# A written order for all five queues, from batch 1's stage 1 to the first channel mixing, in a three-stage kernel on one core

## The chip, the cores and the metric

The kernel runs on 1 core of a Trainium2 chip. The metric is the device time of one execution in microseconds (us). The engines are PE (TensorE matmuls; PEld is its weight load), DVE (VectorE), ACT (ScalarE), POOL (GpSimd) and SP (SyncE, which issues the DMAs). Each engine takes its instructions in one fixed order and stops at the first one whose inputs or buffers are not ready.

## The reference, cut to what matters

```python
def reference(q, k, v, moe, moe2):          # all float32, batch 2, 8 heads, 768 positions, 64 wide
    x = _attn_ref(q, k, v)                   # stage 1: window of 16 and 24 block maxima as keys
    x = x.transpose(0, 2, 1, 3).reshape(2, 768, 512)
    x = _moe_ref(x, **moe)                   # stage 2: 4 experts, best 2 per position
    return _moe2_ref(x, **moe2)              # stage 3

def _moe_ref(x, w_gate, wq, wk, wv, wo):
    ...
    for e in range(E):
        q = x @ wq[e]
        k = x @ wk[e]
        v = x @ wv[e]
        scores = scale * (q @ k.transpose(0, 2, 1))
        scores = np.where(causal, -1000000000.0, scores)
        a = np.exp(scores - scores.max(-1, keepdims=True))
        a /= a.sum(-1, keepdims=True) + 1e-09
        ye = a @ v @ wo[e]
        ...                                  # out += weight of expert e at this position * ye

def _moe2_ref(x, w_tok1, w_tok2, w_ch1, w_ch2):
    xt = x.transpose(0, 2, 1)
    h = np.maximum(xt @ w_tok1, 0.0) @ w_tok2      # token mixing
    u = x + h.transpose(0, 2, 1)
    h2 = np.maximum(u @ w_ch1, 0.0) @ w_ch2        # channel mixing, 1536 wide
    return (u + h2).astype(np.float32)
```

The four weights of stage 3 come as float64 words; the kernel turns their bits into float32 itself ("decode" below).

## The kernel before, in words

All stages are in `stack_kernel`. Exact products are made of three matmuls: `mm3` (lines 112 to 114) multiplies high and low halves, which `split` (L104 on ACT, L105 on DVE) makes from a PSUM tile or from SBUF.

- Stage 1 (`s1_...`, lines 157 to 290): windowed attention, 12 groups per batch. Scores `s1s` (PE, L217), minima `mn` (DVE, L227), exponentials (ACT, L236), scaling (POOL, L252), transposes, value products `s1a` (PE, L271). Batch 0 follows the table FIRST; batch 1 is a generator.
- Stage 2: `proj` makes V, the gate weights `wg` and, in four tiles `pj` per batch and pair of experts, q and k; a tile's halves are called `s...h` and `s...l`, and SP copies them by DMA into q, k and k2l (L449, L450, L453). `attn` runs 8 units per batch (4 experts x 2 halves of the positions). A unit: scores `s2s` (PE, L476), mask and minimum into `pr` and `mn` (DVE, L481), exponential into `pr` with its sum `sm` (ACT, L486), `sm` plus a small number (POOL, L488), reciprocal `f` (DVE, L489), three scalings of `pr` by `f` and `wg` (POOL, L492), transposes `s2p` (PE, L502), split into `ph`/`pl` or copied whole as `pf` (ACT L506), products with V into `s2a` (PE, L507, L512, L513), sum into `yT` (ACT L516, DVE L517).
- Stage 3: `tokmix` makes `yh`/`yl`, `yt`/`nh`/`nl`, `z`, `g` and `u`, tile by tile. `chmix` makes `h` and `o` in four chunks of 384 channels for each batch and half of the positions; the weights of a chunk (`c1h`, `c1l`, `c2h`, `c2l`) come from `load_ch`.
- A decode (`decode_w`, lines 130 to 153) of 128x512 words: DMA into `raw` (L140, SP), absolute value `deca` (ACT, L143), clamp (POOL, L144), three integer steps (DVE, L145 to L147), low word (ACT, L149), product and sum (POOL, L150, L151), high half (ACT, L152), low half (POOL, L153). There are two buffers `raw` and two `deca`, shared by all weights.

Two things set the order. `run` (near line 610) takes turns among generators by their share of work done; after that a scheduler places the traced instructions on each queue as their inputs come, by times of its own. The runs are: stage 1 of batch 1 with `proj(0)`; `attn(0)` with `proj(1)` and the decode of the token weights; `attn(1)` with `tokmix(0)`, the first channel chunk's decode (`load_ch(0)`), the first `chpass` and `tokmix(1)`; then the remaining chunks.

Of the kernel before, what the change touches and what calls it, by code (L numbers as in the profile page):

```python
# [790 lines left out]
```

## Time and profile before

| what | value |
|---|---|
| time, median of 3 runs (lowest to highest) | 466.64 us (465.47 to 469.15) |
| time of the profiled execution | 467.73 us |
| its span (first to last instruction) | 465.9 us |
| granted TensorE clock | 0.998 of full speed |
| PE busy | 445.1 us, 96% of the span |
| PE weight loads busy | 420.7 us, 90% |
| DVE, ACT, POOL busy | 280.1, 231.2, 285.2 us (60, 50, 61%) |

Busy time is the union of an engine's instructions. PE instructions overlap, so a busy PE may still be short of its best rate. A wait is idle time of an engine right before an instruction, put down to the event that came last.

### The profile page before, as it was taken

The page shows a single profiled execution, that of the slowest core. Times are in us where ns is not written, and L with a number is a line of the kernel's source. Part 1 is how long each engine was busy: PE and PEld are TensorE (multiplying, and loading weights), DVE is VectorE, ACT ScalarE, POOL GpSimd, SP SyncE. Part 2 cuts the span into 40 slices and gives each one's busy share as a digit, 9 for nine tenths or more (in the row PEclk, how much of TensorE's full clock was granted, in tenths as well). Part 3 has the DMA queues.
Part 4 walks back from the last instruction along what each step waited for, and adds up shares of the span by engine and source line. Part 5 has one row for each costly group of instructions (what it writes and reads, how often), then busy time and mean ns, then how long its engine had stood idle before and what let it go on. Part 6 is the DMA issues. An engine that isn't in the chain of part 4 may idle for free.

```text
span 465.9 us, 8565 instructions
## 1 busy us (share of the span) xinstructions
PE 445.1 (96%) x3038; PEld 420.7 (90%) x3038; DVE 280.1 (60%) x818; ACT 231.2 (50%) x653; POOL 285.2 (61%) x319
## 2 busy tenths in 40 slices
PE   7899899999989878999999999999999999999996
PEld 7798789989978766897999999999999999999996
DVE  5573766759699679868773743677572673332322
ACT  4685665977778687885664423233323321111010
POOL 4568542768989887997873869877864771000000
PEclk9999999999999999999999999999999999999999
DMA  7999917806515865021111120212121100001111
GB/s 222 275 255 310 289 39 207 182 2 167 127 46 152 210 171 146 3 91 45 45 47 46 66 70 2 84 53 78 58 91 45 62 32 0 1 0 69 68 70 68
DMA packets 28522, 46.51 MB, mean 100 GB/s; under 512 B 2496, under 2 KB 19648, under 8 KB 28480
## 3 DMA queue, kind: packets, MB, share of 16 engines
q1 hardware_dynamic: 28480, 45.97, 35.2%
q8 instruction: 24, 0.39, 0.4%
q14 instruction: 18, 0.15, 0.1%
HBM read 33.38 MB, written 3.15 MB: 78 GB/s over the span
## 4 chain that ended last, share of the span: by engine, by line
PE 68%; DMA 10%; DVE 7%; POOL 4%; ACT 3%; issue 3%; SPq 3%; DVEq 0%; ACTq 0%; POOLq 0%
PE h L113 7%; PE h L112 7%; PE h L114 7%; PE o L112 7%; PE o L113 7%; PE o L114 7%; DMA kx<-in_kwT_dram 5%; PE s1s L217 4%; PE s1a L271 2%; DMA qb<-in_qT_dram 2%; POOL pr L492 2%; PE u L112 2%; PE pj L112 2%; PE u L113 2%; PE u L114 2%
## 5 line engine op out<-in xcount | busy, mean ns | idle before, releaser
L144 POOL TENSOR_SCALAR deca<-deca 128x512 f32<-128x512 f32 x30 | 58.0, 1938 | 10.5 <-ACT deca L143 9.7
L113 PE MATMUL o<-hl,c2h 128*128 128x384 f32 x192 | 64.2, 337 | 0.0
L114 PE MATMUL o<-hh,c2l 128*128 128x384 f32 x192 | 64.0, 336 | 0.0
L108 ACT ACTIVATE hh<-h 128x384 fp32r<-128x384 f32 x48 | 23.3, 490 | 79.4 <-PE h L114 78.8
L109 DVE SCALAR_TENSOR_TENSOR hl<-h,hh 128x384 fp32r<-128x384 f32 x48 | 26.5, 555 | 53.2 <-ACT hh L108 53.2
L605 DVE TENSOR_TENSOR oa<-o,oa 128x384 f32<-128x384 f32 x64 | 31.9, 550 | 38.5 <-PE o L114 38.5
L112 PE MATMUL o<-hh,c2h 128*128 128x384 f32 x192 | 49.4, 336 | 0.0
L236 ACT ACTIVATE pr<-n,mn 128x120 f32<-128x120 f32 x96 | 36.6, 384 | 16.3 <-DVE mn L227 15.8
L150 POOL TENSOR_TENSOR raw<-raw 128x512 f32<-128x512 f32 x30 | 31.3, 1042 | 20.4 <-DVE raw L147 18.6
L492 POOL TENSOR_SCALAR pr<-pr,f,wg 128x128 f32<-128x128 f32 (+5 forms) x48 | 40.1, 849 | 5.1 <-DVE f L489 2.9
L151 POOL TENSOR_TENSOR deca<-deca,raw 128x512 f32<-128x512 f32 x30 | 40.8, 1360 | 1.0
L149 ACT ACTIVATE raw<-raw 128x512 f32<-128x512 uint32 x30 | 20.3, 677 | 36.3 <-DMA raw<-in_ch_dram 25.6
L145 DVE TENSOR_SCALAR deca<-deca 128x512 int32<-128x512 int32 x30 | 27.8, 928 | 14.9 <-POOL deca L144 14.9
L486 ACT ACTIVATE pr<-pr,mn 128x128 f32<-128x128 f32 (+5 forms) x48 | 31.9, 665 | 9.8 <-DVE mn L481 9.7
L113 PEld LDWEIGHTS o<-hl,c2h 128*128 128x128 f32 x192 | 36.0, 188 | 0.3 <-DVE hl L109 0.3
L114 PEld LDWEIGHTS o<-hh,c2l 128*128 128x128 f32 x192 | 36.0, 188 | 0.0
L112 PEld LDWEIGHTS o<-hh,c2h 128*128 128x128 f32 x192 | 34.8, 188 | 0.1
L113 PE MATMUL h<-u0l,c1h 128*128 128x384 f32 x96 | 32.5, 338 | 0.0
L112 PE MATMUL h<-u0h,c1h 128*128 128x384 f32 x96 | 32.4, 338 | 0.0
L114 PE MATMUL h<-u0h,c1l 128*128 128x384 f32 x96 | 32.3, 337 | 0.0
L112 PE MATMUL h<-u1h,c1h 128*128 128x384 f32 x96 | 32.3, 336 | 0.0
L113 PE MATMUL h<-u1l,c1h 128*128 128x384 f32 x96 | 32.3, 336 | 0.0
(207 smaller groups left out, 1315.1 us busy)
## 6 DMA issues: line engine op xcount, KB each, us to landing
raw<-in_ch_dram SPq DMA_DIRECT2D x24, 512.0 KB, 3.5
kx<-in_kwT_dram SPq DMA_DIRECT2D x7, 720.0 KB, 10.0
vx<-in_vw_dram SPq DMA_DIRECT2D x8, 576.0 KB, 11.1
qb<-in_qT_dram SPq DMA_DIRECT2D x16, 192.0 KB, 8.9
raw<-in_tok_dram SPq DMA_DIRECT2D x6, 512.0 KB, 4.6
out_dram<-oa SPq DMA_DIRECT2D x16, 192.0 KB, 2.0
vt<-in_vT_dram SPq DMA_DIRECT2D x4, 384.0 KB, 10.3
rqk<-in_wqkv_dram SPq DMA_DIRECT2D x4, 256.0 KB, 10.2
```

What stands on the lines that cost most here:

```text
L109: vec.scalar_tensor_tensor(lo, src, 0.0, hi.bitcast(F32), op0=ALU.max, op1=ALU.subtract)
L112: ten.matmul(out, lh, rh, start=start, stop=False)
L113: ten.matmul(out, lh, rl, start=False, stop=False)
L114: ten.matmul(out, ll, rh, start=False, stop=stop)
L144: gps.tensor_scalar(af, af, F64_TINY, F64_HUGE, op0=ALU.max, op1=ALU.min)
L145: vec.tensor_scalar(ta, ta, 3, 0x3FFFFFFF, op0=ALU.logical_shift_left, op1=ALU.bitwise_and)
L150: gps.tensor_mul(lf, lf, ef)
L151: gps.tensor_add(af, af, lf)
L236: act.activation(pr[:, i, :], n[:, i, :], AF.Exp, bias=mn[:, i:i + 1], scale=-1.0, accum_out=sm[:, i:i + 1])
L486: act.activation(prs[r], prs[r], AF.Exp, bias=mn[:, r, ci:ci + 1], scale=-1.0, accum_out=sm[:, r:r + 1])
L492: gps.tensor_scalar(prs[r][:, :nk], prs[r][:, :nk], f[:, r:r + 1], wg[:, 3 * h + r, e:e + 1], op0=ALU.mult, op1=ALU.mult)
L605: vec.tensor_add(oa[d], a[:, :HALF], oa[d])
```

## The change: one table that orders all five queues

At the end of `stack_kernel` the traced instructions of each queue are taken in the order in which the program issues them and are chained, one to the next, in the order of a table of numbers. The chain carries no semaphore: it only tells the scheduler which instruction stands behind which. The instructions, the SBUF buffers and the arithmetic are the same; PSUM tiles take their banks in the new order. The table's order differs from the one before from about 63 us of the profile (stage 1 of batch 1) to the first chunk of channel mixing; behind it and ahead of it every queue reads as before.

```diff
+ORDER = {
+    "PE": """
+0-192 253-257 193-216 258-262 281-284 263-265 298-301 217-219 306-311 220-236 269-271 330-332 285 237-244 266-268
...
+    "DVE": """
...
+    "ACT": """
...
+    "POOL": """
...
+    "SP": """
+0-35 39 70 75 38 37 36 40 46-47 41 45 42 44 49 43 48 54 51 50 56 52-53 55 57 60 58-59 61 76 66 63 62 64-65 69 68 77 67
...
+}
...
+    queues = {"PE": ten, "DVE": vec, "ACT": act, "POOL": gps, "SP": nc.sync}
+    traced = list(nc.cur_bb.bb.instructions)
+    for name, table in ORDER.items():
+        mine = [x for x in traced if x.engine == queues[name].engine and type(x).__name__.startswith("Inst")]
+        places = []
+        for run_ in table.split():
+            a, _, z = run_.partition("-")
+            places += range(int(a), int(z or a) + 1)
+        assert sorted(places) == list(range(len(mine))), (name, len(places), len(mine))
+        for a, z in zip(places, places[1:]):
+            tc.add_manual_dep(mine[z], mine[a].name, NOSYNC, reason="keep_in_program_order")
     psa_cm.__exit__(None, None, None)
```

The table takes 107 lines at the top, so a line of the kernel before stands 107 lower in the rows of the changed one (L140 is L247 there, L492 is L599). In the rows below a tile's name ends in its number; `raw64` is the tile called `raw` in the profile, and `pr512`, `pr640`, `pr768` and so on are `pr` of that width.

**SP, where the last copies of k for experts 2 and 3 of batch 1 (`k211`, `k2l11`, from the halves `s111h` and `s111l` of tile `pj1111_2439`) meet the first two loads of channel weights (`raw64_2733`, `raw64_2812`).** Before:

```order
L119 DMA rw512_2346<-in_wo_dram 128x512
L140 DMA raw64_2733<-in_ch1_dram 128x4x256
L140 DMA raw64_2812<-in_ch1_dram 128x4x256
L449 DMA k211_2253<-s111h_2394 64x768
L450 DMA k211_2253<-s111h_2394 64x768
L453 DMA k2l11_2254<-s111l_2395 64x768 x2
L449 DMA k211_2253<-s111h_2394 64x768
L450 DMA k211_2253<-s111h_2394 64x768
L453 DMA k2l11_2254<-s111l_2395 64x768 x2
```

In the change:

```order
L226 DMA rw512_2346<-in_wo_dram 128x512
L557 DMA k211_2253<-s111h_2394 64x768 x2
L556 DMA k211_2253<-s111h_2394 64x768
L560 DMA k2l11_2254<-s111l_2395 64x768
L247 DMA raw64_2733<-in_ch1_dram 128x4x256
L560 DMA k2l11_2254<-s111l_2395 64x768 x2
L556 DMA k211_2253<-s111h_2394 64x768
L247 DMA raw64_2812<-in_ch1_dram 128x4x256
L560 DMA k2l11_2254<-s111l_2395 64x768
```

The first load of channel weights stood ahead of all copies of `s111`; it now stands behind three copies of `s111h` and one of `s111l`, and the second load behind all copies but one.

**POOL, at the second unit of batch 1 (expert 0, second half: `sm2_2629`, `pr512_2631`, `pr640_2632`, `pr768_2633`), whose transposes begin with tile `s2p1010_2667` on PE.** Before:

```order
L488 TENSOR_SCALAR sm2_2629<-sm2_2629 128x3
L492 TENSOR_SCALAR pr512_2631<-pr512_2631,f2_2630,wg_1961 128x512
L492 TENSOR_SCALAR pr640_2632<-pr640_2632,f2_2630,wg_1961 128x640
L492 TENSOR_SCALAR pr768_2633<-pr768_2633,f2_2630,wg_1961 128x768
L144 TENSOR_SCALAR deca_2734<-deca_2734 128x512
L144 TENSOR_SCALAR deca_2813<-deca_2813 128x512
L488 TENSOR_SCALAR sm2_2747<-sm2_2747 128x3
L150 TENSOR_TENSOR raw64_2733<-raw64_2733 128x512
L492 TENSOR_SCALAR pr128_2749<-pr128_2749,f2_2748,wg_1961 128x128
```

In the change:

```order
L251 TENSOR_SCALAR deca_2734<-deca_2734 128x512
L595 TENSOR_SCALAR sm2_2629<-sm2_2629 128x3
L257 TENSOR_TENSOR raw64_2733<-raw64_2733 128x512
L599 TENSOR_SCALAR pr512_2631<-pr512_2631,f2_2630,wg_1961 128x512
L599 TENSOR_SCALAR pr640_2632<-pr640_2632,f2_2630,wg_1961 128x640
L599 TENSOR_SCALAR pr768_2633<-pr768_2633,f2_2630,wg_1961 128x768
L595 TENSOR_SCALAR sm2_2747<-sm2_2747 128x3
L251 TENSOR_SCALAR deca_2813<-deca_2813 128x512
L599 TENSOR_SCALAR pr384_2751<-pr384_2751,f2_2748,wg_1961 128x384
L599 TENSOR_SCALAR pr256_2750<-pr256_2750,f2_2748,wg_1961 128x256
```

The clamp and the product of the first channel weights (`deca_2734`, `raw64_2733`) stood behind the three scalings of this unit; they now stand ahead of them. The scalings of the next unit (`pr128_2749` and on) come in another order.

**ACT, around the copy `pf_2527` of a transposed tile of the last unit of batch 0.** Before:

```order
L104 ACTIVATE s111h_2394<-pj1111_2439 128x384
L104 ACTIVATE ph_2517<-s2p0312_2513 128x384
L516 ACTIVATE tmp_2436<-s2a030_2411 64x384
L143 ACTIVATE deca_2813<-raw64_2812 128x512
L149 ACTIVATE raw64_2812<-raw64_2812 128x512
L486 ACTIVATE pr384_2751,sm2_2747<-pr384_2751,mn2_2746 128x384
L104 ACTIVATE yh0_2584<-yT0_1526 128x768
L506 ACTIVATE pf_2527<-s2p0313_2523 128x384
L104 ACTIVATE ph_2533<-s2p0314_2530 128x256
L104 ACTIVATE ph_2541<-s2p0315_2539 128x128
```

In the change:

```order
L211 ACTIVATE ph_2507<-s2p0311_2503 128x384
L211 ACTIVATE s111h_2394<-pj1111_2439 128x384
L623 ACTIVATE tmp_2436<-s2a030_2411 64x384
L211 ACTIVATE ph_2517<-s2p0312_2513 128x384
L613 ACTIVATE pf_2527<-s2p0313_2523 128x384
L211 ACTIVATE ph_2533<-s2p0314_2530 128x256
L211 ACTIVATE nh0_2621<-yt00_2623 128x256
L211 ACTIVATE yh0_2584<-yT0_1526 128x768
```

Ahead of `pf_2527` the decode's two steps (`deca_2813`, `raw64_2812`), an exponential and the 768-column high half of `yh` are gone; it follows `ph_2517`.

## Rows read from the trace of the kernel before

**Rows 1.** Busy time by stretch: stretch, its length, then each engine, clock, DMA.

```profile
63.40:167.36 103.96, 99.72 (x770) 89.87 (x769) 79.50 (x310) 79.18 (x248) 78.31 (x112) 1.00 0.51 129
167.36:177.93 10.57, 8.06 (x49) 6.04 (x48) 8.42 (x18) 8.33 (x21) 8.71 (x9) 1.00 0.79 190
177.93:222.11 44.18, 40.65 (x249) 35.07 (x249) 36.19 (x96) 33.73 (x83) 39.10 (x37) 1.00 0.18 60
222.11:465.90 243.79, 239.93 (x1391) 237.53 (x1391) 119.89 (x208) 71.51 (x142) 121.62 (x95) 1.00 0.15 50
```

**Rows 2.** Waits of PE, 63.4 to 222.2 us: total, times, longest.

```profile
PE s2a L507 <- ACT pf L506: 1.8, 2, 1.3
PE s1s L217 <- DVE mn L227: 1.0, 1, 1.0
PE u L112 <- DVE u0l L105: 0.9, 1, 0.9
PE z L112 <- DVE mn L481: 0.9, 1, 0.9
...
PE s2s L476 <- issue: 0.6, 1, 0.6
PE s2s L476 <- DMA k2l<-s101l: 0.6, 1, 0.6
PE z L112 <- ACT nh L104: 0.6, 1, 0.6
```

**Rows 3.** Timeline of PE, 165 to 178 us: start, length, line, operation.

```profile
165.27 0.34 PE L113 MATMUL pj<-x1l,wqk1h 128*128 128x384 f32 x1
165.45 0.34 PE L114 MATMUL pj<-x1h,wqk1l 128*128 128x384 f32 x1
...
173.16 0.91 PE L507 MATMUL s2a<-pf,V 128*128 128x384 f32 x2 [1.31 <-ACT pf L506]
...
177.93 0.29 PE L502 MATMUL s2p<-ident,pr 128*128 128x128 f32 x1
```

**Rows 4.** Timeline of ACT, 170 to 173 us.

```profile
170.18 0.68 ACT L143 ACTIVATE deca<-raw 128x512 f32<-128x512 f32 x1
...
171.91 0.83 ACT L104 ACTIVATE yh<-yT 128x768 fp32r<-128x768 f32 x1
172.64 0.47 ACT L506 ACTIVATE pf<-s2p 128x384 f32<-128x384 f32 x1
```

**Rows 5.** Timeline of SP, 163 to 170 us: its DMA issues.

```profile
163.45 2.17 SPq L140 DMA_DIRECT2D raw<-in_ch_dram  x2
169.29 0.47 SPq L449 DMA_DIRECT2D k<-s111h  x1
169.81 0.59 SPq L450 DMA_DIRECT2D k<-s111h  x1
```

**Rows 6.** DMA issues of the page: count, size of one, us to landing.

```profile
raw<-in_ch_dram SPq DMA_DIRECT2D x24, 512.0 KB, 3.5
```

**Rows 7.** Timeline of POOL, 166 to 211 us.

```profile
166.96 2.60 POOL L492 TENSOR_SCALAR pr<-pr,f,wg 128x512 f32<-128x512 f32 x3 [0.38 <-DVE f L489]
169.65 3.81 POOL L144 TENSOR_SCALAR deca<-deca 128x512 f32<-128x512 f32 x2
...
174.89 1.04 POOL L150 TENSOR_TENSOR raw<-raw 128x512 f32<-128x512 f32 x1 [0.82 <-DVE raw L147]
...
210.70 1.70 POOL L492 TENSOR_SCALAR pr<-pr,f,wg 128x128 f32<-128x128 f32 x1 [0.56 <-DVE pl L105]
```

**Rows 8.** Timeline of DVE, 171 to 212 us.

```profile
171.60 0.82 DVE L145 TENSOR_SCALAR deca<-deca 128x512 int32<-128x512 int32 x1 [0.68 <-POOL deca L144]
172.46 0.69 DVE L146 SCALAR_TENSOR_TENSOR deca<-raw,deca 128x512 int32<-128x512 int32 x1
...
174.39 0.42 DVE L147 TENSOR_SCALAR raw<-deca 128x512 int32<-128x512 int32 x1
...
211.22 0.95 DVE L105 TENSOR_TENSOR yl<-yT,yh 128x768 fp32r<-128x768 f32 x1
```

More of the change, by code (lines that the diff above doesn't have):

```diff
@@ new lines @@
+541-546 648-651 547-552 587-595 553-558 596-598 559-568 631-633 611-613 615-616 652-653 599-610 614 617 654-667 619
+634-645 668-679 618 620-621 717-718 721-722 719-720 723-734 758-761 680-682 684-686 762-765 689-691 766-776 683
+817-818 821-822 819-820 694-696 777-779 687 705-716 688 846-854 692-693 697 855-863 698-699 702 735-737 864-867
+739-740 700-701 703 743 704 746-754 905-913 755-757 738 741 780-782 742 744 914-916 784-786 745 917-920 783 789-791
+794-796 823-834 798-799 802 805-810 921-922 787 811-813 958-959 814-816 788 792 835-837 960-963 793 797 800 839-840
@@ new lines @@
+801 964-967 803 843 838 841 868-870 880-882 871-876 804 842 877-879 844 884-886 889-891 883 845 887 993-996 894-896
+898-899 997-998 902 888 892 923-934 893 897 935-937 900-901 903-904 939-940 943 938 968-970 941 946-948 972-974
+949-957 942 944-945 977-979 982-984 986-987 971 975-976 1011-1018 990 980-981 985 1019-1020 988 1021-1022 989 991
+999-1001 1051-1052 1004-1005 1002 1053-1058 992 1008 1003 1006 1023-1024 1007 1009-1010 1075-1084 1025-1027 1030-1032
+1085-1086 1035-1037 1131-1133 1028 1134-1139 1040-1042 1029 1033 1149-1152 1044-1045 1153-1154 1048 1059-1060 1034
@@ new lines @@
+1038-1039 1043 1179-1181 1046 1061-1062 1047 1049 1063-1065 1050 1068-1069 1191-1192 1140-1142 1066 1072 1143-1145
+1067 1070 1087-1092 1193-1196 1146-1148 1093-1095 1182-1184 1197-1198 1105-1107 1071 1096-1101 1108 1102-1104
+1110-1112 1115-1117 1109 1199-1200 1120-1122 1113-1114 1124-1125 1239-1241 1251-1252 1128 1155-1157 1253-1254
+1158-1160 1242-1244 1118-1119 1123 1255-1256 1126 1073-1074 1127 1167-1169 1129 1293-1298 1161-1166 1245-1247
+1299-1301 1185-1187 1130 1172-1173 1176 1201-1209 1188-1190 1213-1215 1218-1220 1248-1250 1302-1304 1170-1171 1174
@@ new lines @@
+1305-1306 1175 1177 1307-1308 1178 1309-1310 1210-1212 1311-1312 1223-1225 1216 1269-1280 1313-1314 1228-1230
+1232-1233 1217 1221-1222 1236 1353-1364 1226 1257-1259 1227 1231 1281-1283 1234-1235 1237 1367-1369 1284 1238
+1370-1372 1285 1373-1375 1286-1287 1290 1260-1268 1315-1320 1288 1327-1329 1332-1334 1289 1291-1292 1321-1326
+1337-1339 1330 1342-1344 1331 1381-1382 1335-1336 1376-1378 1346-1347 1350 1365-1366 1379-1380 1340-1341 1345
+1348-1349 1351 1383-1391 1352 1399-1401 1392-1394 1402-1407 1397-1398 1413-1415 1422-1424 1408-1410 1395-1396
@@ new lines @@
+1411-1412 1440-1448 1500-1505 1449-1454 1416-1421 1455-1457 1425-1439 1458-1475 1479-1481 1476-1478 1506-1508
+1482-1493 1512-1514 1545-1553 1515-1520 1509-1511 1521-1529 1557-1559 1530-1532 1581-1592 1560-1568 1494-1499
+1533-1544 1593-1595 1605-1607 1596-1604 1638-1640 1569-1571 1617-1622 1629-1631 1623-1628 1572-1580 1608-1616
+1641-1643 1647-1652 1665-1667 1644-1646 1653-1655 1554-1556 1668-1676 1656-1658 1677-1688 1701-1703 1659-1664
+1689-1691 1719-1721 1710-1712 1737-1739 1692-1697 1749 1698-1700 1632-1637 1740-1747 1713-1715 1748 1750 1704-1709
@@ new lines @@
+1751-1758 1716-1718 1759-1760 1722-1733 1761-1773 1782 1791 1800 1774-1775 1783-1784 1792-1793 1801 1776 1785 1794
+1802-1803 1777-1778 1786-1787 1795-1796 1804 1779 1788 1797 1805 1780-1781 1789-1790 1798-1799 1806-1821 1734-1736
+1822-1845 1854 1863 1872 1846-1847 1855-1856 1864-1865 1873 1848 1857 1866 1874-1875 1849-1850 1858-1859 1867-1868
+1876-1877 1851 1860 1869 1878 1852-1853 1861-1862 1870-1871 1879-1916 1953-1956 1917 1926 1935 1944 1918-1919 1927
+1920 1928-1929 1936 1921-1922 1930-1931 1937-1940 1945-1946 1923 1932 1941 1947 1924-1925 1933-1934 1942-1943
@@ new lines @@
+1948-1952 1957-1989 1998 2007 1990-1991 1999-2000 2008-2009 2016-2017 1992 2001 2010 2018 1993-1994 2002-2003
+2011-2012 2019-2020 1995 2004 2013 2021-2022 1996-1997 2005-2006 2014-2015 2023-2061 2070 2079 2062-2063 2071-2072
+2080-2081 2088-2089 2064 2073 2082 2090 2065-2066 2074-2075 2083-2084 2091-2093 2097-2100 2067 2076 2085 2094
+2068-2069 2077-2078 2086-2087 2095-2096 2101-2133 2142 2151 2160 2134-2135 2143-2144 2152-2153 2161 2136 2145 2154
+2162 2137-2138 2146-2147 2155-2156 2163-2164 2139 2148 2157 2165 2140-2141 2149-2150 2158-2159 2166-2205 2214 2223
@@ new lines @@
+2206-2207 2215-2216 2224-2225 2232-2233 2208 2217 2226 2234 2209-2210 2218-2219 2227-2228 2235-2237 2241 2211 2220
+2229 2238 2212-2213 2221-2222 2230-2231 2239-2240 2242-2277 2286 2295 2278-2279 2287-2288 2296-2297 2304-2305 2280
+2289 2298 2306 2281-2282 2290-2291 2299-2300 2307-2308 2283 2292 2301 2309 2284-2285 2293-2294 2302-2303 2310-2349
+2358 2367 2350-2351 2359-2360 2368-2369 2376-2377 2352 2361 2370 2378 2353-2354 2362-2363 2371-2372 2379-2380 2355
+2364 2373 2381 2356-2357 2365-2366 2374-2375 2382-2421 2430 2439 2422-2423 2431-2432 2440-2441 2448-2449 2424 2433
@@ new lines @@
+2442 2450 2425-2426 2434-2435 2443-2444 2451-2452 2427 2436 2445 2453 2428-2429 2437-2438 2446-2447 2454-2493 2502
+2511 2494-2495 2503-2504 2512-2513 2520-2521 2496 2505 2514 2522 2497-2498 2506-2507 2515-2516 2523-2524 2499 2508
+2517 2525 2500-2501 2509-2510 2518-2519 2526-2565 2574 2583 2566-2567 2575-2576 2584-2585 2592-2593 2568 2577 2586
+2594 2569-2570 2578-2579 2587-2588 2595-2596 2571 2580 2589 2597 2572-2573 2581-2582 2590-2591 2598-2637 2646 2655
+2638-2639 2647-2648 2656-2657 2664-2665 2640 2649 2658 2666 2641-2642 2650-2651 2659-2660 2667-2668 2643 2652 2661
@@ new lines @@
+2669 2644-2645 2653-2654 2662-2663 2670-2672
+""",
+    "DVE": """
+0-84 94-95 85-87 96-99 114 88-89 109-112 103 121 115 122-124 90 116 129 91 104 120 113 125 108 92 100 134-136 93
+101-102 126 105 137 127 106 128 107 147 138 133 148 130 142-145 139 149-150 140-141 131-132 117 146 118-119 171
+166-168 151 157 164 152-153 158 154 169 155-156 165 170 177 159-163 173-176 185 178 180-183 188 184 172 186-187 179
+189-193 195-199 201-204 208-211 205-206 212 219 194 200 207 213 220-221 214 222 215 223 216 224 235 217-218 236
@@ new lines @@
+225-226 237-238 231 228 286 239 287-288 295 227 232-233 240 229 234 241 296 242-244 230 253-255 297 266 257 267-269
+258-259 270 302 256 303 245 298 300 285 304 271 299 246 316-318 247-248 319 250 320 301 306-307 251-252 260 249 261
+263 308 321 264-265 273 262 289 272 334-335 290 278-279 274-276 312 305 336 291 343 277 294 344-345 280 337 281-283
+346-347 292 309 313-315 284 310 293 333 348 322 326-327 354 311 356 328-329 355 323-325 338 357 330 339-340 349 342
+341 350 331 365-367 351 368 332 358 369 378 364 382-384 352 360 379-381 370 361-362 353 396-397 371 395 399 385 363
@@ new lines @@
+372 398 400 373-374 392 415 393 401 375-376 413-414 386-388 427 394 359 428-429 389 377 430 390 403 416 409 402 404
+431 405 410-412 444-445 432 406 446 407 391 419 417 424-425 418 426 408 447 420-421 472 423 440 458 434 459 422 461
+435 460 441 433 454 442-443 462 449 436-437 471 463 438 450 455-456 439 451-452 457 448 465-466 453 464 467 507-508
+468-469 509 476-477 474-475 470 478 473 480-481 479 482 512-514 483 485 484 486-489 517 523 518-519 524-525 492
+528-529 491 490 496 493-494 498 530 499 501 497 500 503-504 495 506 505 533-534 553-555 535 502 510-511 515-516 520
@@ new lines @@
+522 558-559 526 560 527 563-565 531-532 536-537 521 538 569 539 570-571 540 574-576 541-546 579-581 547 599-600
+548-549 601 550-552 556 604-606 557 561-562 566-568 572-573 609-610 577-578 582 611 583 615 584 616-617 585-587 620
+588-589 621 590 622 591 625-627 592-598 602-603 607-608 612-614 618-619 623-624 628-657
+""",
+    "ACT": """
+0-69 76-79 85 84 87 86 70-72 93 91-92 73-74 80 88 94 75 81 96 82 97 83 95 102 101 104 100 98 112-113 106 108 105 107
+99 103 89 109 90 114 111 116 118-120 110 117 115 121-122 124-126 123 128 127 130 129 134 136 133 132 131 135 137 139
@@ new lines @@
+141 140 142 145 147 146 148 153-154 151-152 169 138 143 149 144 159 150 156 155 161 160 157-158 162 170 164 163
+171-172 165-166 173 167 174 168 214 183 180 176-177 225 184 215 185 175 181 226 178 182 186 216 187-188 179 198-199
+201 231 200 202 232 210 189 211 190 209 213 228 227 191-192 229 235-236 230 242 193-194 203 196 246-247 195 197
+204-205 248 207 233 208 217 206 218-220 243 261-262 244 212 234 237 221 251 224 263 270 222 238-239 250 271-272 260
+240 223 253 249 254-255 241 245 256-257 280 258 282 281 264-265 259 266-267 273 252 274 269 268 275-277 289 283 290
@@ new lines @@
+412 443 416-417 445 435 449 448 424 428 452 451 429 450 456 455 436 453 437 461 460 438 457 464 463 439 462 440 474
+441 473 465 442 478-479 446-447 482 486 454 458 475 480 459 481 485 466-467 483 468 491 490 487 494 493 469-470 492
+471 495 472 476-477 484 488-489 496-507
+""",
+    "POOL": """
+0 2 1 3-41 48 50 56 63-64 57 49 42 51 43 55 46-47 52 54 53 44-45 58 62 59-61 70 65 68 67 66 69 71 76 73 80 77 79 74 72
+75 78 81 84-85 82-83 86-87 91 89 88 90 92 94 93 95-97 101 98 103 100 104 107 106 99 105 102 108 111 109 112 110 113
@@ L49 @@
+262 252 263 267-269 264-266 271 270 275 272-273 276 274 277 279 278 283 280-281 284 282 285 287 286 288 291 289-290
+292 295 293 296-297 294 298-299 303 300-301 304 302 305 307 306 311 308-309 312 310 313-314
+""",
+    "SP": """
+0-35 39 70 75 38 37 36 40 46-47 41 45 42 44 49 43 48 54 51 50 56 52-53 55 57 60 58-59 61 76 66 63 62 64-65 69 68 77 67
+86-87 73 71 78 72 74 80-81 79 85 82 84 92 90 88 91 93 83 89 99 95 94 96 102 97 101 98 103 100 104-141
+""",
+}
 F64_TINY = 2.0 ** -15
```

14 lines of the change are left out of this document (added).

## The prediction

> **What bounds the kernel now.** I read the page first (PE busy 445.1 of 465.9 us), then the busy time by stretch, then the waits of PE, then the timelines around the largest waits. The stretches are cut where the new order acts [rows 1]. From 222.11 us on PE has no named wait left, and its idle rest of 243.79 - 239.93 = 3.86 us lies in slots between matmuls; nothing there can be won, because the order of the channel mixing stays. Between 63.40 and 222.11 us PE is idle for 103.96 - 99.72 = 4.24 us, then 10.57 - 8.06 = 2.51 us, then 44.18 - 40.65 = 3.53 us: 10.28 us together. By the waits view this is no single cause but a score of short waits, most of them for a split or a copy by ACT or DVE, a few for a DMA [rows 2]. So PE's order binds in all stretches, and an engine that serves it late opens a hole.
>
> A wait costs more than its idle time. In an unbroken row the 384-column matmuls start 0.18 us apart although each lasts 0.34 us [rows 3]; after a hole this overlap of 0.16 us is lost once. In the timeline there are 8 waits of at least 0.15 us in the first stretch, 4 in the second and 7 in the third. What PE has to do between two points of an order I count from the rows of the order at this step: 0.18 us for 384 columns, others in proportion.
>
> **What the change does, part by part.** No instruction is added or removed, so each effect is a wait that goes or comes. I went through the 19 waits and asked of each what now stands ahead of the late instruction on its own engine, and how much PE work lies between the matmul that triggers it and the one that uses it.
>
> Term 1, 63.40 to 167.36 us: six of the eight waits lose their cause. The 1.0 us for the minima of stage 1 and the two waits at the copies of `k2l`, 0.6 us each [rows 2], get more PE work in front (for the minima 4.0 instead of 2.2 us); SP now issues `k2l` two places earlier. Three more, for `mn`, a `pf` and a `ph`, have a shorter queue ahead of them. The other two (0.66 us together) I count by half. That is 4.24 - 0.33 = 3.9 us, and 7 x 0.16 = 1.1 us of overlap: -5.0 us. From below it is bounded by nothing won, from above by 4.24 + 8 x 0.16 = 5.5 us.
>
> Term 2, 167.36 to 177.93 us. One by one the four waits here would go: the 1.31 us wait [rows 3] is for `pf` on ACT, ahead of which stood steps of a decode and the high half of `yh`, 0.68 and 0.83 us among them [rows 4], and the new order of ACT puts them behind it. But the same order makes a new chain. SP issued the first channel weights at 163.45 us, ahead of the copies of `s111` that began at 169.29 us [rows 5]; now they stand behind four of these, so they start after the last tile `pj`. POOL has to clamp and multiply them before it scales the probabilities of the second unit, which `s2p` needs at 177.93 us [rows 3]. From the end of `pj` (167.36 us): high half of `s111` 0.48, four issues at about 0.6 as spaced in rows 5, 2.4, landing 3.5 [rows 6], ACT's `deca` 0.68 [rows 4], POOL's clamp 3.81 / 2 = 1.9 [rows 7], DVE's three steps 0.82 + 0.69 + 0.42 = 1.93 [rows 8], POOL's product 1.04 and the three scalings 2.60 [rows 7]: 14.5 us, and 0.45 us for seven hand-overs makes 15.0 us, where before it took 10.57 us. Before, the scalings ended at 166.96 + 2.60 = 169.56 us, 8.4 us ahead of their use. PE now does some work in this piece that stood ahead of `pj`: 16 score and transpose matmuls with 4864 columns, 2.3 us; so it comes to `pj` that much earlier. It also does 4 matmuls with 1280 columns from behind it, 0.6 us. Net: 15.0 - 10.57 - 2.3 - 0.6 = +1.5 us. Without this chain the term would be -2.51 - 4 x 0.16 = -3.2 us. At the long end, with 1.7 us for a scaling that else takes 0.45 (below) and issues at 0.9, it is +4.0 us. I take +1.5, as each piece is a row.
>
> Term 3, 177.93 to 222.11 us: of 3.53 us I leave 0.2 us at the 0.9 us wait of `z` for DVE (the `yl` that stood ahead is gone, but a service of about 1.5 us has 1.3 us of cover) and 0.4 us of the 0.6 us of `z` for `nh` (its cover grows only from 2.6 to 2.8 us); the 0.9 us of `u` [rows 2] goes, since its bank now comes from an earlier tile and a decode step no longer stands ahead on DVE. 2.95 us and 6 x 0.16 = 1.0 us of overlap: -3.9 us. Bounds: nothing, and 3.53 + 7 x 0.16 = 4.7 us.
>
> Term 4, waits that the trace of before can't show. A unit's lead is the PE work between its last scores and its first transpose. It shrinks in all eight units of batch 1: from 9.4 to 4.0 us in the second, 12.1 to 8.4 in the third, 15.2 to 11.7 in the sixth, 20.8 us in sum. Most had slack, such as the 8.4 us above. The second is term 2; the third stands behind the same late decode, on POOL and on ACT, and loses 3.7 us of lead. Between nothing and 3.7 us I take half: +1.9 us.
>
> Durations are as before, with one doubt. A 128-column scaling on POOL took 1.70 us at 210.70 [rows 7], elsewhere mostly 0.45; it ended 0.2 us behind a DVE subtraction of two SBUF tiles that ran from 211.22 to 212.17 us [rows 8]. Here the trace agrees with the Trainium skill ("SBUF — State Buffer", section "Who interferes with whom"): a DVE instruction with two SBUF inputs and a GpSimd instruction that reads SBUF exclude each other for a whole instruction. By it a new order draws these 1.25 us anew at other pairs; I leave the sum as it is.
>
> Sum: -5.0 + 1.5 - 3.9 + 1.9 = -5.5 us against the profiled execution's 467.73 us (span 465.9 and 1.83 around it), so 462.2 us. The median of the runs lies 1.09 us below that execution: 461.1 us.
>
> **Rivals.**
> A, the late decode rules (slower): the first channel weights come even later than I worked out, and the units behind them have no lead left to hide it. Term 2 is then +4.0 us, term 4 3.7 us, and term 3 brings nothing because PE would only arrive earlier at the same probabilities: -5.0 + 4.0 + 3.7 = +2.7 us, 469.3 us by the median. For it: the eight shorter leads (term 4). Against it: POOL had 8.4 us to spare at the second unit. It turns the sign once the stalls and lost gains at these units exceed those of my sum by 5.5 us.
> B, the chain hides itself: PE's leftover work covers the decode, all four waits go and no new ones come: -5.0 - 3.2 - 3.9 = -12.1 us, 454.5 us. For it: every wait was too short to need a new place for more than one instruction. Against it: the 15.0 us are all on one chain.
> C, the waits only move: each engine's sum of work is the same, and what was late for one tile is late for the next: about 466 us. For it: POOL was busy 39.10 of 44.18 us in the third stretch [rows 1]. Against it: it was not what PE waited for there [rows 2].
> That the table changes nothing is excluded: the orders differ on all five queues.
>
> **How the numbers follow.** The forecast has 0.58 (own range 457.5 to 465), A 0.15, B 0.12, C 0.15. About 1%, 4.7 us, can be told from no change: below 461.97 us is faster, above 471.3 us slower. Of the forecast two thirds (0.39) lie under 461.97, with B 0.51 for faster. A goes over 471.3 us where POOL's scalings fall on DVE's subtractions too: 0.10 of its 0.15; with 0.02 of the forecast's, for a wait on a PSUM bank that I missed, slower has 0.12. The rest, 0.37 (0.17 of the forecast, 0.05 of A, all of C), is within 1%. The range runs from B's time to just over A's: 454.5 to 470.
>
> **What would show it.** Right: the wait of 1.0 us for stage 1's minima and those for `k2l` are gone; PE stands 5 to 7 us (15.0 less the 8.4 us of work that it then has in that piece) in one or two waits just ahead of the second unit's transposes; its busy time from the first chunk of channel mixing is the same. Wrong: no wait at that unit (B), or waits of `s2p` at three units and more (A), or 10 us of idle in other places (C).

## The result, and the profile after

The changed kernel took 473.13 us (median of 4 executions, 470.28 to 475.95), the kernel before 467.25 us in the same comparison: a ratio of 1.0142, 95% interval 1.0096 to 1.0188. It is slower by 5.9 us (1.4%), where 5.5 us less were forecast. The profiled execution took 474.31 us.

The page of the changed kernel: span, PE's busy time, and the granted clock of TensorE in 40 slices of 11.8 us (9 is full speed).

```profile
span 472.5 us, 8564 instructions
...
PE 450.6 (95%) x3038; PEld 426.8 (90%) x3038; DVE 275.6 (58%) x818; ACT 232.8 (49%) x653; POOL 284.6 (60%) x319
...
PEclk9999999779999995999999999999999999999999
```

In the profile of the kernel before every slice had a 9. Here the clock falls twice. The same by stretch (stretch, its length, then PE, PEld, DVE, ACT and POOL busy, clock, DMA):

```profile
63.40:86.40 23.00, 22.33 (x215) 21.03 (x213) 16.44 (x96) 17.74 (x75) 13.75 (x40) 1.00 0.80 188
86.40:89.80 3.40, 0.01 (x1) 0.01 (x1) 0.95 (x3) 0.75 (x4) 0.48 (x2) 0.89 0.24 55
89.80:99.70 9.90, 9.90 (x79) 8.35 (x81) 2.93 (x12) 5.34 (x19) 3.40 (x8) 0.52 0.01 2
...
173.20:188.00 14.80, 8.96 (x34) 6.76 (x35) 9.81 (x31) 10.16 (x27) 8.44 (x9) 0.66 0.40 99
188.00:222.10 34.10, 32.97 (x216) 30.40 (x215) 27.42 (x75) 26.88 (x68) 30.01 (x32) 1.00 0.14 48
222.10:472.50 250.40, 243.89 (x1414) 240.60 (x1412) 124.85 (x219) 75.72 (x150) 132.45 (x101) 1.00 0.16 53
```

PE does nothing for 3.40 us, and then works for 9.90 us at a granted clock of 0.52, which is 1.2 GHz nearly all the time. From 173.2 us it idles 5.8 of 14.8 us, at a mean clock of 0.66. The waits of PE behind 63 us (total, times, longest), against [rows 2]:

```profile
PE s2a L620 <- DVE pl L212: 4.5, 3, 2.8
PE s1a L378 <- DVE x1l L389: 3.4, 1, 3.4
PE u L219 <- DVE u1l L212: 1.0, 1, 1.0
PE o L220 <- DVE hl L216: 1.0, 1, 1.0
PE yt L642 <- DVE yT L624: 1.0, 1, 1.0
PE s2a L619 <- ACT ph L211: 0.9, 1, 0.9
...
PE s2s L583 <- DMA k<-s101h: 0.8, 1, 0.8
```

Of the waits in [rows 2], those for the minima of stage 1, for `k2l`, `pf` and both of `z` are gone. In their place stand a few long ones, and 0.8 us for the copy of `k` from the tile s101, where the wait for its `k2l` stood before.

To see where time goes and comes from I take PE's instructions in their order, count the work ahead of each at the steps of [rows 3], and subtract this from the time at which it starts. What is left is lost time; its growth between two amounts of work, in us (an estimate: some 410 us of work in all by this count; each column one profiled execution; b0 is a second profile of the kernel before, a1 and a10 are experiments below):

| work done, us | before | b0 | after | a1 | a10 |
|---|---|---|---|---|---|
| 0 to 32 | 7.6 | 6.8 | 6.4 | 7.4 | 7.2 |
| 32 to 70 | 8.5 | 8.5 | 4.2 | 4.0 | 4.0 |
| 70 to 82 | 2.7 | 2.6 | 12.0 | 3.8 | 3.8 |
| 82 to 136 | 12.0 | 12.0 | 10.4 | 10.7 | 10.7 |
| 136 to 148 | 8.4 | 8.4 | 12.3 | 13.0 | 8.7 |
| 148 to 196 | 8.9 | 9.4 | 7.2 | 6.9 | 9.9 |
| 196 to 400 | 1.9 | 2.1 | 4.2 | 4.5 | 4.7 |

The first row is chance: it holds the waits for the first loads, which differ from one execution to the next. The new order gains 4.3 us from 32 to 70 and 3.3 us in two later rows. It loses 9.3 us at one place and 3.9 us at another, and 2.3 us in the channel mixing.

**The first place** is no term of the forecast. DVE and PE of the changed kernel around it (start, length, line, operation, idle time before and what ended it):

```profile
84.82 0.17 DVE L351 RECIPROCAL ri<-sm 128x4 f32<-128x4 f32 x1
88.85 0.56 DVE L212 TENSOR_TENSOR s010l<-pj,s010h 128x384 fp32r<-128x384 f32 x1 [3.87 <-DMA k<-s001h]
89.33 0.74 DVE L389 TENSOR_TENSOR x1l<-s1a,x1h 128x256 fp32r<-128x256 f32 x2
```

```profile
85.74 0.65 PE L364 MATMUL s1p<-ident,pr 128*120 128x128 f32 x4
89.80 0.48 PE L378 MATMUL s1a<-pTs,vx 120*64 120x64 f32 x4 [3.40 <-DVE x1l L389]
```

DVE stands for 3.87 us before the low half of the tile s010 (L212). It overwrites a buffer from which SP's copies of s001 still read. Behind it wait the low halves `x1l`, and for the first of these PE's `s1a`, which needs the PSUM bank. The order before had the next three `x1l` (85.56, 89.50 and 91.37 us) ahead of this instruction, and ran it at 92.64 us without a wait for the copies.

**The second place** is term 2. POOL, ACT, DVE and PE there:

```profile
176.85 1.92 POOL L251 TENSOR_SCALAR deca<-deca 128x512 f32<-128x512 f32 x1 [8.61 <-ACT deca L250]
...
180.62 1.05 POOL L257 TENSOR_TENSOR raw<-raw 128x512 f32<-128x512 f32 x1 [1.22 <-DVE f L596]
181.65 2.60 POOL L599 TENSOR_SCALAR pr<-pr,f,wg 128x512 f32<-128x512 f32 x3
```

```profile
176.09 0.67 ACT L250 ACTIVATE deca<-raw 128x512 f32<-128x512 f32 x1 [1.77 <-DMA raw<-in_ch_dram]
...
180.61 0.68 ACT L250 ACTIVATE deca<-raw 128x512 f32<-128x512 f32 x1 [1.33 <-DMA raw<-in_ch_dram]
...
181.89 0.48 ACT L623 ACTIVATE tmp<-s2a 64x384 f32<-64x384 f32 x1
```

```profile
178.80 0.43 DVE L252 TENSOR_SCALAR deca<-deca 128x512 int32<-128x512 int32 x1 [1.60 <-POOL deca L251]
179.26 0.69 DVE L253 SCALAR_TENSOR_TENSOR deca<-raw,deca 128x512 int32<-128x512 int32 x1
...
180.48 0.59 DVE L212 TENSOR_TENSOR pl<-s2p,ph 128x256 fp32r<-128x256 f32 x2
```

```profile
180.93 0.58 PE L620 MATMUL s2a<-pl,V 128*128 128x256 f32 x1 [2.82 <-DVE pl L212]
...
183.02 0.47 PE L642 MATMUL yt<-ident,yT 128*128 128x128 f32 x1 [0.95 <-DVE yT L624]
...
186.16 1.06 PE L609 MATMUL s2p<-ident,pr 128*128 128x128 f32 x4
```

POOL waits 8.61 us for the decode of the first channel weights, whose load SP issued at 169.54 us, and scales the second unit's probabilities only behind it, until 184.25 us. PE does not wait for these: it comes to their transposes (L609) at 186.16 us and starts at once. Its waits lie ahead of that. The longest, 2.82 us, is for `pl`, which stands on DVE behind the same decode (L252 to L254). On ACT the second load's decode (180.61 us) stands ahead of `tmp`, on which `yT` and PE's `yt` depend.

### The profile page after: what moved, and what is told of

Its sections match the earlier page's. It is cut to its first block, busy times and chain, and to the rows that moved or that the text cites. A ratio compares the mean times of both kernels' runs of the same rounds, so it can differ in the third digit from the quotient of the medians.

```text
span 472.5 us, 8564 instructions
## 1 busy us (share of the span) xinstructions
PE 450.6 (95%) x3038; PEld 426.8 (90%) x3038; DVE 275.6 (58%) x818; ACT 232.8 (49%) x653; POOL 284.6 (60%) x319
## 5 line engine op out<-in xcount | busy, mean ns | idle before, releaser
L251 POOL TENSOR_SCALAR deca<-deca 128x512 f32<-128x512 f32 x30 | 59.8, 1995 | 22.9 <-ACT deca L250 22.1
L219 PE MATMUL o<-hh,c2h 128*128 128x384 f32 x192 | 50.9, 336 | 0.0
L257 POOL TENSOR_TENSOR raw<-raw 128x512 f32<-128x512 f32 x30 | 31.8, 1059 | 20.7 <-DVE raw L254 16.0
L343 ACT ACTIVATE pr<-n,mn 128x120 f32<-128x120 f32 x96 | 36.7, 384 | 12.1 <-DVE mn L334 10.4
L599 POOL TENSOR_SCALAR pr<-pr,f,wg 128x256 f32<-128x256 f32 (+5 forms) x48 | 37.5, 789 | 2.5 <-DVE f L596 1.7
L252 DVE TENSOR_SCALAR deca<-deca 128x512 int32<-128x512 int32 x30 | 24.5, 819 | 20.6 <-POOL deca L251 20.6
L256 ACT ACTIVATE raw<-raw 128x512 f32<-128x512 uint32 x30 | 20.3, 677 | 30.8 <-DMA raw<-in_ch_dram 24.9
L221 PE MATMUL h<-u1h,c1l 128*128 128x384 f32 x96 | 32.3, 337 | 0.0
```

What stands on the lines that cost most here:

```text
L219: ten.matmul(out, lh, rh, start=start, stop=False)
L221: ten.matmul(out, ll, rh, start=False, stop=stop)
L251: gps.tensor_scalar(af, af, F64_TINY, F64_HUGE, op0=ALU.max, op1=ALU.min)
L252: vec.tensor_scalar(ta, ta, 3, 0x3FFFFFFF, op0=ALU.logical_shift_left, op1=ALU.bitwise_and)
L257: gps.tensor_mul(lf, lf, ef)
L343: act.activation(pr[:, i, :], n[:, i, :], AF.Exp, bias=mn[:, i:i + 1], scale=-1.0, accum_out=sm[:, i:i + 1])
```

## The experiments

A kernel of the a series takes the table and moves some instructions of a queue to behind another; the line of each diff gives queue, instructions (numbers of the table) and the one they go behind. Ratios are to the kernel before, run on the same chip in the same job.

| run | median us | ratio, 95% interval |
|---|---|---|
| b0_before | 468.5 | 1.0014, 0.9977 to 1.0052 |
| a1_split_behind | 467.08 | 0.9998, 0.9965 to 1.0031 |
| a2_load_ahead | 473.9 | 1.0129, 1.0076 to 1.0182 |
| a3_both | 468.9 | 1.0034, 1.0004 to 1.0065 |
| a4_filled | 471.65 | 1.0092, 1.0061 to 1.0124 |
| a5_both_loads | 466.97 | 0.9978, 0.9942 to 1.0015 |
| a6_unit_first | 469.45 | 1.0033, 1.0002 to 1.0063 |
| a7_loads_unit | 469.43 | 1.0046, 1.0012 to 1.0081 |
| a8_decode_behind | 468.03 | 1.0014, 0.9975 to 1.0052 |
| a9_and_tail | 474.29 | 1.0112, 1.0053 to 1.017 |
| a10_next_decode | 467.32 | 1.0011, 0.9979 to 1.0043 |
| a11_last_pl | 468.45 | 1.0018, 0.9984 to 1.0052 |
| h1_old_from_140 | 466.78 | 0.9989, 0.996 to 1.0019 |
| h2_old_from_152 | 467.62 | 0.9985, 0.9952 to 1.0019 |
| h3_old_tail | 473.93 | 1.0145, 1.0102 to 1.0187 |
| h4_old_tail_later | 473.0 | 1.0113, 1.0063 to 1.0164 |

**The control.** The kernel before, unchanged.

> The kernel before, once more, for a second profile. It tells which differences of the traces are the runs' own: both theories expect the time of before within 1%, no granted clock under 0.95 in any 20 us from 63 us on, and a start (0 to 63 us) that may differ by 1 to 2 us.

It took 468.5 us. Its table of lost time agrees with the first profile within 0.8 us in each row, so I take larger differences there as the orders' own. Its clock is not that of the first profile. Behind a wait of 2.73 us (2.29 us in the first profile) it was 0.50 from 47.9 to 51.3 us:

```profile
47.83 0.76 PE L217 MATMUL s1s<-kx,qb 128*128 128x120 f32 x2 [2.73 <-DVE mn L227]
```

```profile
PEclk9999899999999999999999999999999999999999
```

So the order before isn't free of this loss either. The 126 executions of it beside the experiments have mean granted clocks of 0.982 to 1.000, with a median of 0.993; the one that the forecast was read from had 0.998, which 13 of them reach.

**The first hole, and the clock by itself.**

```diff
+MOVES = [("DVE", [219], 213)]        # a1: low half of s010 behind the fourth x1l
...
+        for at, n in FILL.get((b, hp, g), ()):      # a4, in s1_turn: FILL = {(1, 3, 0): ((512, 16),)}
+            for _ in range(n):
+                fills.append((at, ten.matmul(pT[:, :P], ident, ident, start=True, stop=True).ins))
```

> The new order with one move on DVE: the low half of s010 (which overwrites a buffer that DMAs still read) goes behind the four low halves x1l instead of ahead of them. Theory 'hole and clock': the 3.4 us hole of PE at 86.4 us goes, and with it the half clock of 89.5 to 100 us (about 10.3 us of work at half speed, 5.2 us lost): 473.1 - 8.6 = 464.5 us. Rival 'idle alone': only the hole counts, 469.7 us. Rival 'the wait moves': 472 to 473 us.

> The new order, untouched, with 16 matmuls more on PE (identity times identity into a PSUM tile that is overwritten afterwards) ahead of the instruction that waits at 86.4 us, so that PE is busy while it waits. Theory 'hole and clock': the wait is as long as before, but the clock stays at its higher level: 473.1 - 5.2 = 467.9 us, with granted clock 1.00 from 80 to 100 us. Rival 'idle alone', in which the clock falls for another reason: 473 us, clock 0.5 from 89.5 us as before.

a1: one move on DVE takes the loss at the first place from 12.0 to 3.8 us and the ratio from 1.0142 to 0.9998, 6.7 us of the 8.6 expected. Its time alone, 467.08 us, lies midway between 'hole and clock' (464.5) and 'idle alone' (469.7) and doesn't decide between them. a4 leaves the wait (3.81 us on DVE) and keeps PE busy during it:

```profile
89.40:93.20 3.80, 3.76 (x32) 3.65 (x32) 1.22 (x3) 0.64 (x3) 0.37 (x2) 1.00 0.21 49
93.20:103.00 9.80, 9.80 (x124) 8.27 (x125) 3.06 (x12) 6.20 (x21) 4.87 (x10) 1.00 0.01 2
```

```profile
89.44 3.84 PE L368 MATMUL s1p<-ident 128*128 128x128 f32 x32 [0.16 <-ACT pTs L375]
93.21 0.69 PE L384 MATMUL s1a<-pTs,vx 120*64 120x64 f32 x16
```

L368 are the 16 added products (32 instructions in the trace), into a PSUM tile that is overwritten afterwards. The clock stays at 1.00. From the first `s1a` behind the hole to the first transpose of stage 2, at 104.8 us in the changed kernel and 104.1 us here, it takes 104.8 - 89.8 = 15.0 us without and 104.1 - 93.2 = 10.9 us with them: 4.1 us by the traces. In a1, without the hole, the same piece takes 97.4 - 86.5 = 10.9 us too. By the ratios it is 0.5%, 2.3 us; the intervals overlap, so that the times alone would not show it, and 471.65 us is nearer to the rival's 473 than to the 467.9 us expected. What decides is the clock: 1.00 behind the wait in a4's trace, and a mean over the span of 0.984 to 0.993 in its six executions, against 0.974 to 0.982 in the four of the change. The place and the wait are the same and only PE's idleness is gone, so the half clock follows from the idle PE.

**The second hole: the loads.**

```diff
+MOVES = [("SP", [102], 89)]                                            # a2
+MOVES = [("DVE", [219], 213), ("SP", [102], 89)]                       # a3
+MOVES = [("DVE", [219], 213), ("SP", [102], 89), ("SP", [103], 96)]    # a5
```

> The new order with one move on SP: the first load of channel weights (raw64_2733) goes ahead of the copies of s111, as it stood before. Theory 'hole and clock': the four holes between 174 and 184 us (0.92 + 1.07 + 2.82 + 0.95 = 5.8 us) go for the most part, and the half clock of 178 to 188 us (6.2 us of busy PE, 3.1 us lost) goes: 473.1 - 6 to 8.9, about 465.5 us. Rival 'idle alone': 467.3 us. Rival 'short leads': the unit has too little work ahead of it in any case, 471 us or more.

> Both moves together. Theory 'hole and clock': the savings add up, 456 to 460 us, under the kernel before. Rival 'the rest of the new order is slower too': 466 us or more.

> The DVE move of a1_split_behind, and on SP both first loads of channel weights ahead of copies of s111: raw64_2733 ahead of all, raw64_2812 behind the fourth. Theory 'the late loads make the second hole': the wait of yt for yT (3.9 us in a3_both, where ACT stood at the second load's decode ahead of tmp) goes, what is left are waits of 1 us, and the clock stays: 467.1 - 3.9 - 3 = about 460 us. Rival 'it is the rank of the decode on ACT, POOL and DVE': 465 us or more.

All three missed; the figure of a rival came each time ('short leads' for a2, 'the rest of the new order is slower too' for a3, the rank of the decode for a5). With the first load early (a2, a3) the wait only went to the next consumer. a3, on ACT, DVE and PE:

```profile
176.66 0.67 ACT L255 ACTIVATE deca<-raw 128x512 f32<-128x512 f32 x1 [4.15 <-DMA raw<-in_ch_dram]
...
177.88 0.48 ACT L628 ACTIVATE tmp<-s2a 64x384 f32<-64x384 f32 x1
...
178.40 0.56 DVE L629 TENSOR_TENSOR yT<-s2a,tmp 64x384 f32<-64x384 f32 x1 [4.32 <-ACT tmp L628]
...
179.01 0.47 PE L647 MATMUL yt<-ident,yT 128*128 128x128 f32 x1 [3.94 <-DVE yT L629]
```

The second load's decode holds ACT 4.15 us until its DMA lands; `tmp`, `yT` and `yt` follow, and PE idles 3.94 us. With both loads early (a5) there are still four waits of 0.9 to 1.7 us between 170 and 179 us and a clock of 0.70 from 170 to 180 us.

**The second hole: the rank of the decode.** These kernels put the decode's steps behind the units' own, on ACT, POOL and DVE.

```diff
+MOVES = [("DVE", [219], 213),                                          # a6
+    ("ACT", [302, 303, 305, 306], 292), ("ACT", [314, 315], 284),
+    ("POOL", [179, 180], 178), ("POOL", [187], 184), ("DVE", [379, 380, 381], 362)]
...
+    ("SP", [102], 89), ("SP", [103], 96),                              # a7: a6 and these
...
+    ("POOL", [179], 178), ("POOL", [180, 181], 184), ("POOL", [187], 181),
+    ("DVE", [379, 380, 381], 395)                                      # a8: a7 with these instead
...
+    ("DVE", [392, 393], 388)                                           # a10: a8 and this
+    ("DVE", [507, 508], 469)                                           # a11: a10 and this
+    ("DVE", [507, 508], 469), ("DVE", [528, 529, 530], 501)            # a9: a8 and these
```

> The DVE move of a1_split_behind, and at the second and third unit of batch 1 the decode steps of the first two channel weights go behind the units' own steps on ACT, POOL and DVE; SP's loads stay late. Theory 'late loads' and theory 'rank' agree that the holes of PE go, since nothing that PE waits for stands behind the loads: 467.1 - 6 (holes) - 3 (half clock) = 458 to 460 us. Rival 'short leads': the unit's own chain of 7.5 us against 4 us of work leaves 3 us of holes, 463 us or more.

> All moves of a5_both_loads and a6_unit_first together. Theory 'late loads': as a6_unit_first, and the decode comes earlier, so that POOL's later stretch gains: 457 to 459 us. Rival: the earlier loads hold back the copies of s111 and the time is that of a6_unit_first or 1 to 2 us more.

> As a7_loads_unit, and DVE's three steps of the first load's decode go further back, behind the sum yT of the last unit of batch 0 (in a7_loads_unit yT stood 5.7 us behind them, as they wait for POOL's clamp, which stands behind three scalings), with POOL's product behind the third unit's scalings. Theory 'decode ahead of the units': no wait over 1.5 us between 150 and 190 us and no half clock there, 467.1 - 6 = about 461 us. Rival 'short leads': the wait goes to s2p of the second or third unit, 465 us or more.

> As a8_decode_behind, and DVE's first two steps of the second load's decode (deca_2813) go behind the scores and splits that followed them (in a8_decode_behind they waited 3.2 us for POOL at 182 us, and PE's u behind them 2.5 us, with a half clock). Theory 'a decode step ahead of a split on DVE makes the hole': no wait over 1.5 us from 100 us on, granted clock 1.00 there, 468.0 - 3 = 465 us. Rival 'the hole only goes on to the next consumer': 467 us or more and again one wait over 2 us.

In a6 and a7 PE stood 4.7 and 5.7 us at `yt`. The reason in a7 is one DVE step:

```profile
172.52 1.92 POOL L262 TENSOR_SCALAR deca<-deca 128x512 f32<-128x512 f32 x1
174.47 0.43 DVE L263 TENSOR_SCALAR deca<-deca 128x512 int32<-128x512 int32 x1 [3.96 <-POOL deca L262]
...
176.12 0.56 DVE L635 TENSOR_TENSOR yT<-s2a,tmp 64x384 f32<-64x384 f32 x1
...
176.73 0.48 PE L653 MATMUL yt<-ident,yT 128*128 128x128 f32 x1 [5.70 <-DVE yT L635]
```

DVE's first decode step needs POOL's clamp, which I had put behind three scalings; the sum `yT` stood behind it. a8 mends this and has no wait over 1.1 us up to 186 us, but there the next decode does the same:

```profile
183.17 1.91 POOL L263 TENSOR_SCALAR deca<-deca 128x512 f32<-128x512 f32 x1
...
185.11 0.43 DVE L264 TENSOR_SCALAR deca<-deca 128x512 int32<-128x512 int32 x1 [3.16 <-POOL deca L263]
...
185.46 0.55 DVE L600 CUSTOM_DVE_ANT_0 pr<-s2s,cmask 128x384 f32<-128x384 f32 x1
```

PE's `u` waited 2.46 us behind that. a10 moves this step too. Its trace has no wait over 1.3 us from 100 to 300 us, and the loss from 136 to 148 us of work is 8.7 us, about that of the kernel before (8.4). So each hole of over 2 us at this place, in the change and in a2 to a8, had a decode step that stood ahead of a split or a sum and waited for POOL or a DMA. The time, however, stayed at a ratio of 1.0011, and the clock was not 1.00 all along as expected. The table shows where the gain went: of the 4.3 us that a10 has over a1 from 136 to 148 us of work it loses 3.0 again from 148 to 196, with new waits of 1.0 and 1.2 us for DVE's `mn` (L601):

```profile
177.43 0.39 PE L232 MATMUL z<-t1h,nh 128*128 128x256 f32 x1 [0.98 <-DVE mn L601]
...
189.25 0.33 PE L596 MATMUL s2s<-k,q 128*128 128x128 f32 x1 [1.17 <-DVE mn L601]
```

By time none of a6, a7, a8 and a10 met its theory; the rival's time came each time, though in a10 without the long wait that its rival named.

> As a8_decode_behind, and two decodes more on DVE go behind splits that PE waits for: that of deca_3903 behind the last pl of the units (wait of 0.6 to 0.8 us at 236 us) and that of deca_4090 behind u1l (1.0 us at 269 us). Theory 'each hole counts once': a8_decode_behind less 1.7 us. Rival: the decode of later weights comes late, no gain.

> As a10_next_decode, and the decode steps of deca_3903 on DVE go behind the last pl of the units, without the second move of a9_and_tail (which brought the wait of 5.7 us for c1h). Theory: the 0.75 us wait of s2a at 236 us and what follows it go, 1.4 us under a10_next_decode, about 463.6 us. Rival: no difference.

a9 took the wait of 0.75 us at 236 us away and paid 5.7 us at 286 us, where `h` then waited, on a decode moved too far back. a11 made no difference, as its rival had it: the wait at 236 us went, and that of `u` for `u1l` grew from 1.08 to 2.04 us.

**Old and new in one table.** The h series follows a new order up to a time of its trace and the order before behind that; all five sections of the table are written anew.

```diff
 ORDER = {
...
-    "PE": (the order of the change)
+    "PE": (what a1 had begun by 135 us, then the rest as before)      # h1; h2: by 147 us
+    "PE": (what a10 had begun by 222 us, then the rest as before)     # h3; h4: by 228 us
```

> A table again, but of two parts: all that a1_split_behind had begun by 135 us of its trace in its order, and the rest of all five queues in the order of the kernel before (which had done that much by 140 us). Theory 'the new order is better up to there and loses it at the second and third unit': 467.1 of a1_split_behind (or 468 of before) less 4 to 5 us, about 463 us, no wait over 1.5 us behind 100 us. Rival 'a lead is used up later': the old order behind it waits for the same things, 466 us or more.

> As h1_old_from_140, cut at 147 us of the trace of a1_split_behind (152 us of before). Theory as there: 463 us. Rival as there: 466 us or more.

> A table of two parts: all that a10_next_decode had begun by 222 us of its trace in its order, the rest of all queues in the order of the kernel before. Theory 'the new order gains ahead of the channel mixing and loses in it': the three waits of 0.7 to 1.1 us behind 222 us go, and the time is that of a10_next_decode (467.3) less 3, about 464 us, some 3 to 4 under before. Rival 'the seam makes a hole of its own', as in h1 and h2: 466 us or more.

> As h3_old_tail, cut at 228 us of the trace of a10_next_decode. Theory: 464 us. Rival: 466 us or more.

All four missed their theory, and their rivals' figure came. The seam made a hole each time: 2.33 us in h1, 2.23 us in h2, 7.79 us in h3 and 7.14 us in h4. So h1 and h2 are level with before, h3 and h4 as slow as the change. Whether the new order's lead at 222 us could be kept by a better joint is open. No version here beats the kernel before by more than its interval.

## Why the prediction was wrong

- **The step that failed** is the search for waits. I asked of each old wait what now stands ahead of it; a new wait at an instruction that had none I only looked for at the units (terms 2 and 4). DVE's low half of s010, on a buffer that DMAs still read, is such a one. With the half clock behind it, it cost 8.2 us of lost time (12.0 in the change against 3.8 in a1) and 6.7 us by the ratios, and it turned the sign: with this one instruction moved the new order is level with the kernel before (0.9998). The rest of the miss, about 5 us, is in the points below.
- **What bounds the kernel.** PE's order does bind, as read. But I took PE's step as constant, since the clock was 1.00 in all of [rows 1]. The half clock stands in no term: it cost 4.1 us at the first hole by a4's trace; for the second there is no such run. That [rows 1] had 1.00 throughout was chance, as b0 shows.
- **Where the orders part.** I had the stretch up to 63.40 us unchanged, and the channel mixing too. In the traces DVE's order differs from 46.4 to 310.3 us of the kernel before and PE's from 48.2 to 313.0 us. The first instruction of PE that moves ran behind a wait of 2.29 us; this wait is gone. That is most of the 4.3 us from 32 to 70 us of work, and no term had it.
- **Term 1** (-5.0 us). Besides the new hole, the gain was sized too high. In the table a1, without the hole, stands 4.7 us under the kernel before from 32 to 136 us of work; two waits ahead of 63.40 us (2.29 and 0.36 us) are 2.65 of it, so that some 2 us are left of the 5.0 (an estimate). The wait for the minima went, as worked out. At the copies of s101 PE stood 1.2 us before; of the two waits that I read there as `k2l` the trace puts one to `k2l` and one to "issue" [rows 2]. It still stands there 0.8 us in the change and 1.1 us in a1, now for `k`.
- **Term 2** (+1.5 us). The late load was right, the way from it to PE was not, and the size was +3.9 us of lost time. The load landed at 176.09 us, 6.5 us from its issue instead of 3.5, among the copies, so that POOL's scalings ended 17.7 us behind the end of `pj` (166.51 us) instead of 15.0. PE came to the second unit's transposes only 19.65 us behind it, at 186.16 us, and did not wait for POOL there. It was held by `pl` and `yT`, behind the decode on DVE and on ACT, where I had followed it only through POOL; and it ran the end at half clock. That its idle time, 5.8 us, lies in the 5 to 7 us that I gave as a sign is luck: it is four waits at other instructions.
- **Term 3** (-3.9 us). 1.7 us came, from 148 to 196 us of work; in a10 nothing came there.
- **Term 4** (+1.9 us, for shorter leads). It stays open. In a10, with the decode steps behind and the leads unchanged, no wait over 1.3 us was left at these units, but the waits of PE from 167 to 225 us still add up to 6.1 us. No run lengthens a lead by itself.
- **The channel mixing** was to stay. It lost 2.3 us: in the list of waits above, 1.0 us for `u1l` and 1.0 us for `hl`. The first (276.23 us) lies where the orders still differ. The second (353.95 us) lies where all queues read as before; why it comes is not shown.
- **Rivals.** A had the direction and the late decode, at 469.3 us; it lacked the first hole and the clock. B did not happen. C, that the waits only move, gave 466 us and not the time of the change, but it fits the runs without the first hole: they are within 1% of the kernel before, but for a9, h3 and h4, and each long wait that was taken away came back at another consumer.

## What to carry to other kernels

When an order is rewritten, don't only ask which old waits go: go through every instruction that now stands earlier and needs a DMA, a buffer that a DMA reads, or a step of a slower engine, and see who is queued behind it. In the change the long hole of PE cost more than its idle time, because the clock fell with it; in the first profile of the kernel before the many short waits left it at 1.00, and in the second one wait of 2.73 us did not. And when a decode moves, follow it on every engine: of the single moves here most only handed the hole to the next consumer. Moving its steps on all engines (a10) took the long holes away, but no time.

## What the runs showed of the hardware that I had not expected

The granted clock fell to 0.50 at 89.1 us, within the 3.40 us without work that began at 86.4 us, and stayed there until 99.3 us although PE was busy from 89.8 us on. In a10 it was 0.50 for 3.4 us only, from 171.5 to 174.9 us, with no single wait over 1.1 us ahead of it. Holes of 1.31 us [rows 3] and 2.29 us in the first profile of the kernel before left it at 1.00; behind one of 2.73 us, in b0, it was 0.50 for 3.4 us. At the start, 0.50 for 3.4 us followed a first hole of 2.1 us (a1, 10.9 us), and none followed one of 1.07 us (the change). That may be part of why executions of one kernel differ (470.28 to 475.95 us for the change): over the 126 executions of the kernel before, time and mean granted clock have a correlation of -0.67. No run here tests it.

A DVE step of the decode that took 0.43 us at 178.80 us of the change (L252 there) took 1.23 us beside POOL's additions, in a1 (L256):

```profile
266.25 4.55 POOL L697 TENSOR_TENSOR oa<-u0h,u0l 128x384 f32<-128x384 f32 x4
266.31 1.23 DVE L256 TENSOR_SCALAR deca<-deca 128x512 int32<-128x512 int32 x1 [7.07 <-POOL deca L255]
...
267.58 1.39 DVE L257 SCALAR_TENSOR_TENSOR deca<-raw,deca 128x512 int32<-128x512 int32 x1
...
268.89 1.94 DVE L216 TENSOR_TENSOR u1l<-u,u1h 128x384 fp32r<-128x384 f32 x4
...
269.49 0.45 PE L223 MATMUL u<-yh,woh 128*128 128x384 f32 x1 [1.01 <-DVE u1l L216]
```

Both DVE steps are long (L257 took 0.69 us at 179.26 us of the change, as L253), the low halves `u1l` stand behind them, and PE waits 1.01 us. The Trainium skill ("SBUF — State Buffer", section "Who interferes with whom") says that a DVE instruction in a two-port mode or with two SBUF inputs and a GpSimd instruction that reads SBUF exclude each other for whole instructions; the trace agrees for L257, which reads two and is 0.7 us longer. L256 reads one and is 0.8 us longer; whether it ran in such a mode no row shows. No run here varies it by itself.
